# Borrowed PSUM banks at the outset, joined runs of small matmuls, inputs' loads on GpSimd's queue, and a last tile stored in halves, in a feed-forward plus S4 convolution kernel

## The chip, the cores and the metric

The kernel runs on one core of a Trainium2 chip. The metric is the device time of one launch in microseconds (us), the median of several launches. Engines are named as the profile names them: PE is TensorE, DVE VectorE, ACT ScalarE, POOL GpSimd, SP SyncE. SP, ACT and POOL also issue DMA transfers, each on a queue of its own; PSUM is the small memory that PE writes its results to, in banks, and SBUF the memory that all engines work from.

## The reference

The output is the input plus two branches of its layer norm: an S4 convolution over the sequence and a feed-forward network with silu.

```python
def _A_ref(u, A_re, A_im, B_re, B_im, C_re, C_im, log_dt, Dskip):
    dt = jnp.exp(log_dt)[:, None]
    logdA = dt * (A_re + 1j * A_im)
    dB = dt * (B_re + 1j * B_im)
    P = jnp.exp(logdA[:, :, None] * l[None, None, :])
    K = jnp.einsum("dn,dnl,dn->dl", Cc, P, dB).real
    ...
    y = irfft(rfft(u, padded) * rfft(K, padded))[:L]
    return y + u * Dskip

def _B_ref(x, w1, w2):
    return einsum("bsf,fd->bsd", silu(einsum("bsd,df->bsf", x, w1)), w2)

x = A_u
xn = _layernorm(x, axis=-1)
return x + _A_ref(xn, ...) + _B_ref(xn, B_w1, B_w2)
```

The sequence has L = 2048 rows of D = 576 columns, the hidden width F is 4608, each column has N = 128 complex states.

## The kernel before

**The feed-forward network** carries the bulk of TensorE's work. Every float32 factor is split into a high and a low part that TensorE takes at its fast float32 rate, and a product is the sum of three: high by high, high by low, low by high. The sequence is cut into four blocks of 512 rows, two to a half; the hidden width into nine chunks of four slices t = 0 to 3, 128 wide. For each half, each chunk and each of its two blocks:

- `up(blk, t)` (L305) makes one slice of the hidden layer: 14 matmuls into one bank `ph` (L313 to L315) from the transposed inputs xh, xl, x4 and the weights w1h, w1l; then ACT reads the bank with silu into gf (L321) and makes gh, its high part (L322), and DVE makes gl, its low part (L323). `ph` lies in the pool ps1, of two banks.
- `down(blk, jj)` (L325) multiplies by w2: for each 128-row tile, 12 matmuls for each of the two column halves into a bank `po` of the pool ps2, of three banks (L338), then DVE adds the bank to the accumulator acc (L342).

Only the first block's ups are done in two halves of 256 columns, all four t with columns 0 to 256 first (a = 0, e = 256), then all four with 256 to 512, since its second half of inputs arrives later.

**The outset** is what must happen before that runs: `load_x` (L162) brings tiles of 128 input rows, two at a time (tiles 0 and 1 apart), `phase0` (L204) and `norm` (L179) normalise them (statistics on DVE at L186, the power on POOL at L191, the result xn on DVE at L195 or on ACT at L200), and `put_xt` (L120) transposes them on PE (L124, L128) and splits them into xh on ACT (L125) and xl on DVE (L126). `load_w1` (L253) and `split_w1` (L272), `load_w2` (L286) and `split_w2` (L294) bring the weights and split them, the high part on ACT (L280, L300), the low part on DVE (L282, L302). `idle(n)` issues n matmuls of zeros (L857), which nobody reads, while the first inputs arrive.

**The side work** makes the convolution by a transform and is woven between the feed-forward matmuls. `kgen()` (L562) makes the convolution's kernel K in 18 rounds: DVE and ACT compute tables S and C, PE multiplies them in a run of 128 matmuls `kp` of 32-column tiles (L674), ACT copies the result to kt (L681), PE transforms it in a run of 16 matmuls `z` of 64-row tiles (L689), ACT copies these to `stage` (L697), and every second round SP stores `stage` to d1k in HBM (L702). `spread()` (L139) makes the inputs' transform in 16 steps j with two halves m each: the load xr (L145), a split sp on ACT and DVE (L150, L151), matmuls pu (L155, L156), the copy u1 on ACT (L157), and a store to d1u on POOL's queue (L158). `spectral()` (L708) reads d1k and d1u back and multiplies. `next_xt` (L349) loads the second half's transposed inputs on POOL's queue (L352, L355) and `split_xt` (L358) splits them. `tail()` and `add_conv` bring the convolution into acc, and `store` (L174) writes the tiles out; the last two tiles, 14 and 15, are written by the last lines of the program, each in four parts over SP and ACT.

**The order.** Each engine and each queue works through its instructions in the order in which the build put them, and a queue's transfer starts when its wait is met. The build's scheduler chooses this order from the program's, with a plan of times of its own. The kernel steers it with `behind(ins)`: what is issued inside stands behind the instruction `ins`, without a wait for it; the dictionary `pins` holds such instructions. `weave` hands the side work out among the feed-forward matmuls by marks.

## Time and profile before

| | |
|---|---|
| median of 3 runs | 1113.24 us (1112.6 to 1115.7) |
| the profiled execution | 1113.42 us, of which the span is 1111.6 |
| granted TensorE clock | 1.00 |
| PE busy | 1103.3 us, 99% of the span |
| DVE, ACT, POOL busy | 82%, 64%, 6% |
| moved by DMA | 148.56 MB, mean 134 GB/s |

The time is that of the launch; the span is what the profiler saw, from the first instruction to the last, and the difference lies around it. PE busy is the union of its matmuls' times, so a matmul that runs below its pace because the array changes its tiling counts as busy. Rows of a timeline give the start, the duration, the engine and line, the operation with its output and inputs, and in brackets the idle time ahead of it and what ended it. A run of like matmuls is folded into one row with its count; its duration is from the first start to the last end. The costliest groups by line are these: columns are the line, the engine and operation, the names, shapes and count, then busy us and mean ns, then the idle time just before them.

```profile
L338 PE MATMUL po<-w2l,gh 128*128 128x288 f32 x1152 | 338.5, 295 | 0.9 <-DVE w2l L302 0.9
L313 PE MATMUL ph<-xh,w1h 128*128 128x512 f32 (+1 forms) x592 | 162.1, 388 | 1.2 <-ACT gf L321 1.2
L674 PE MATMUL kp<-C 128*32 128x64 f32 x1152 | 35.2, 222 | 0.0
L689 PE MATMUL z<-f,kt 64*128 64x128 f32 x288 | 20.9, 285 | 0.0
```

### The profile page before, as it was taken

How to read it: one execution, taken by the hardware profiler on the slowest of the kernel's cores; microseconds unless marked ns; L12 is line 12 of the kernel's file. 1: busy time of each engine (PE TensorE's matmuls, PEld its weight loads, DVE VectorE, ACT ScalarE, POOL GpSimd, SP SyncE). 2: the span in 40 equal slices, each digit the busy share in tenths (PEclk: the TensorE clock that was granted, in tenths of full speed). 3: DMA queues.
4: the chain of work that ended last, by engine and by line, in shares of the span. 5: the costliest groups of instructions: out<-in, count | busy, mean ns of one | idle time of the engine just before them, and what ended most of it. 6: DMA issues, size and time to landing. Idle time of an engine off the chain costs nothing.

```text
span 1111.6 us, 22913 instructions
## 1 busy us (share of the span) xinstructions
PE 1103.3 (99%) x9168; PEld 997.8 (90%) x9168; DVE 916.9 (82%) x1546; ACT 709.2 (64%) x1228; POOL 69.8 (6%) x129
## 2 busy tenths in 40 slices
PE   8999999999999999999999999999999999999998
PEld 6998999899889899899989989999999999999887
DVE  6899899999999999999999837787778778784433
ACT  5574456676777676677866536877777878773210
POOL 1100000000000000011000000000000000000111
PEclk9999999999999999999999999999999999999999
DMA  9745522425242515255844163554545445434983
GB/s 258 201 122 152 137 71 61 120 63 130 82 107 80 134 61 131 77 149 161 219 123 105 44 173 106 169 157 128 161 145 150 139 146 171 129 107 130 248 211 86
DMA packets 175563, 148.56 MB, mean 134 GB/s; under 512 B 111024, under 2 KB 142272, under 8 KB 175328
## 3 DMA queue, kind: packets, MB, share of 16 engines
q1 hardware_dynamic: 165136, 112.33, 38.7%
q0 software_dynamic: 9568, 33.62, 9.5%
q8 instruction: 72, 1.18, 0.5%
q10 hardware_dynamic: 752, 1.15, 0.4%
q14 instruction: 35, 0.29, 0.1%
HBM read 102.53 MB, written 44.61 MB: 132 GB/s over the span
## 4 chain that ended last, share of the span: by engine, by line
PE 97%; DMA 1%; DVE 0%; SPq 0%; issue 0%; ACT 0%; ACTq 0%; POOL 0%; DVEq 0%
PE po L338 42%; PE ph L313 35%; PE kp L674 3%; PE ph L314 3%; PE ph L315 3%; PE pu L804 2%; PE pb L804 2%; PE pk L804 2%; PE z L689 2%; PE pu L155 1%; DMA acc<-in_A_u_dram 1%; PE py L825 1%; PE pu L156 1%; DMA w2r<-in_B_w_dram 0%; PE pt L124 0%; DVE st L186 0%
## 5 line engine op out<-in xcount | busy, mean ns | idle before, releaser
L338 PE MATMUL po<-w2l,gh 128*128 128x288 f32 x1152 | 338.5, 295 | 0.9 <-DVE w2l L302 0.9
L338 PE MATMUL po<-w2h,gl 128*128 128x288 f32 x1152 | 336.2, 295 | 0.0
L338 PE MATMUL po<-w2h,gh 128*128 128x288 f32 x1152 | 335.8, 295 | 0.0
L338 PEld LDWEIGHTS po<-w2h,gh 128*128 128x128 f32 x1152 | 215.1, 188 | 7.6 <-issue 2.8
L338 PEld LDWEIGHTS po<-w2l,gh 128*128 128x128 f32 x1152 | 215.9, 188 | 6.1 <-DVE w2l L302 1.1
L338 PEld LDWEIGHTS po<-w2h,gl 128*128 128x128 f32 x1152 | 215.4, 188 | 0.8
L321 ACT ACTIVATE gf<-ph 128x512 f32<-128x512 f32 (+1 forms) x148 | 86.4, 585 | 142.9 <-PE ph L315 128.3
L313 PE MATMUL ph<-xh,w1h 128*128 128x512 f32 (+1 forms) x592 | 162.1, 388 | 1.2 <-ACT gf L321 1.2
L313 PE MATMUL ph<-xl,w1h 128*128 128x512 f32 (+1 forms) x592 | 161.4, 386 | 0.0
L313 PE MATMUL ph<-xh,w1l 128*128 128x512 f32 (+1 forms) x592 | 161.0, 385 | 0.0
L342 DVE TENSOR_TENSOR acc<-po,acc 128x288 f32<-128x288 f32 x288 | 126.4, 452 | 37.4 <-PE po L338 36.1
L323 DVE TENSOR_TENSOR gl<-gf,gh 128x512 fp32r<-128x512 f32 (+1 forms) x148 | 99.2, 673 | 64.8 <-ACT gh L322 64.1
L313 PEld LDWEIGHTS ph<-xh,w1l 128*128 128x128 f32 x592 | 108.1, 188 | 19.9
L313 PEld LDWEIGHTS ph<-xl,w1h 128*128 128x128 f32 x592 | 108.0, 188 | 20.0 <-DVE xl L126 0.2
L313 PEld LDWEIGHTS ph<-xh,w1h 128*128 128x128 f32 x592 | 104.5, 188 | 18.5 <-ACT gf L321 1.8
L322 ACT CAST gh<-gf 128x512 fp32r<-128x512 f32 (+1 forms) x148 | 89.8, 609 | 10.1 <-PE po L338 7.1
L631 ACT ACTIVATE c<-th,magic 128x1040 f32<-128x1040 f32 x36 | 42.1, 1169 | 37.9 <-DVE C L654 28.0
L633 ACT ACTIVATE c<-th 128x1040 f32<-128x1040 f32 x36 | 38.7, 1075 | 34.0 <-DVE th L632 34.0
L300 ACT CAST w2h<-w2r 128x576 fp32r<-128x576 f32 x72 | 46.9, 671 | 17.2 <-PE po L338 14.9
L282 DVE TENSOR_TENSOR w1l<-w1r,w1h 128x640 fp32r<-128x640 f32 x72 | 57.1, 818 | 0.2
L314 PE MATMUL ph<-x,w1h 128*128 128x512 f32 (+1 forms) x148 | 57.0, 385 | 0.0
L315 PE MATMUL ph<-x,w1l 128*128 128x512 f32 (+1 forms) x148 | 56.9, 385 | 0.0
(184 smaller groups left out, 1830.1 us busy)
## 6 DMA issues: line engine op xcount, KB each, us to landing
w2r<-in_B_w_dram SPq DMA_DIRECT2D x72, 288.0 KB, 3.7
w1r<-in_B_w_dram SPq DMA_DIRECT2D x35, 512.0 KB, 3.9
d1u<-u POOLq DMA_DIRECT2D x32, 288.0 KB, 2.6
d1k<-stage SPq DMA_DIRECT2D x18, 512.0 KB, 6.8
ur<-d1u SPq DMA_DIRECT2D x32, 288.0 KB, 3.9
kr<-d1k SPq DMA_DIRECT2D x32, 288.0 KB, 2.8
d<-yo POOLq DMA_DIRECT2D x32, 288.0 KB, 3.7
ys<-d SPq DMA_DIRECT2D x32, 288.0 KB, 11.6
```

What stands on the lines that cost most here:

```text
L282: pins["w1l"] = nc.vector.tensor_sub(l1, src, h1).ins
L300: pins["w2h"] = nc.scalar.copy(h2, r2).ins
L313: nc.tensor.matmul(ph, w[:, kt, :], v[:, kt, a:e], start=n + kt == 0, stop=False)
L314: nc.tensor.matmul(ph, h1[:, 4, :], x4[:, a:e], start=False, stop=False)
L315: pins["pe"] = nc.tensor.matmul(ph, l1[:, 4, :], x4[:, a:e], start=False, stop=True).ins
L321: nc.scalar.activation(gf, ph, AF.Silu)
L322: pins["gh"] = nc.scalar.copy(gh, gf).ins
L323: pins["gl"] = nc.vector.tensor_sub(gl, gf, gh).ins
L338: pins["pe"] = nc.tensor.matmul(po[:, :HD], G[blk, t][g][:, js], W2[half, c, t][w][:, hs], start=n == 0, stop=n == 3 * FT - 1).ins
L342: nc.vector.tensor_add(acc[j][:, hs], po[:, :HD], acc[j][:, hs])
L631: nc.scalar.activation(c65, th, AF.Identity, bias=magic)
L804: nc.tensor.matmul(dst, st, mv[:, hs], start=n == 0, stop=n == 3 * len(terms) - 1)
```

## The change

Seven things are changed.

- `up`: the first halves of the slices t = 2 and 3 of the first block put `ph` into a bank of ps2, which the `po` of the downs use, rather than of ps1.
- `norm`: tile 3 is normalised on DVE (L195) rather than on ACT (L200), so its mb on DVE falls away.
- The loads of tiles 2 and 3 are issued on SP alone rather than on SP and ACT; of the first slices of w1, the two 64 KB rows that POOL issued go to SP and ACT. Eight idle matmuls rather than nine follow tile 0.
- What stands behind what: tiles 2 and 3 behind the latest w1l rather than the first; the w1l of slices 2 and 3 behind other steps of `norm`; the statistics of tiles 6 and 7 behind the latest w2l rather than the transposes of tile 3; the late tiles 8 and 9 behind an xn.
- `kgen`: the z run of a round is issued by `along` right behind the kp run of the next round rather than behind its own; kt gets two buffers; the last round's z stands alone.
- `spread`: the loads xr move from SP's queue to POOL's, and two steps are taken at every second round rather than one at each.
- `store`: tile 15 is written in two column halves, each in four parts over SP and ACT.

In the order that the build makes of it, 17 kp runs are followed directly by a z run, and the last z run stands in two parts with four matmuls of an up between them. On POOL's queue the load xr of step j + 1 stands between the two stores d1u of step j. Directly ahead of block 1's first up stand the five transposes of tile 7, where before 12 matmuls of a down stood between the fourth and the fifth. The last tile's stores are eight of 36 KB rather than four of 72 KB.

```diff
--- before.py
+++ after.py
@@ -142,7 +142,7 @@
         nc.gpsimd.dma_start(s1, cs1)
         for j in range(NJ):
             src = up.tile([P, D], F32, tag="xr", name="xr")
-            nc.sync.dma_start(src, dxn[:, j])
+            nc.gpsimd.dma_start(src, dxn[:, j])
             for m in range(2):
                 lo, hi = slice(64 * m, 64 * m + 64), slice(64 - 64 * m, 128 - 64 * m)
                 u1 = up.tile([P, D], F32, tag="u1", name="u1")
@@ -173,8 +173,9 @@
 
     def store(t, j, engines):
 
-        for ps, v, eng in quarters(ov, engines):
-            eng.dma_start(v[:, j:j + 2] if len(t.shape) > 2 else v[:, j], t[ps])
+        for hs in (slice(0, HD), slice(HD, D)) if j == NJ - 1 else (slice(0, D),):
+            for ps, v, eng in quarters(ov, engines):
+                eng.dma_start(v[:, j:j + 2] if len(t.shape) > 2 else v[:, j, hs], t[ps] if len(t.shape) > 2 else t[ps, hs])
 
     def norm(p0, js, xs):
 
@@ -187,11 +188,11 @@
             nc.vector.bn_aggr(out=mv[:, i, :], in_=st[:, i, :, :])
         sd = p0.tile([P, 2], F32, tag="sd", name="sd")
         mb = p0.tile([P, 2], F32, tag="mb", name="mb")
-        nc.vector.tensor_scalar(sd[:, :n], mv[:, :n, 1], 1e-5, None, op0=ALU.add)
+        pins["sdv"] = nc.vector.tensor_scalar(sd[:, :n], mv[:, :n, 1], 1e-5, None, op0=ALU.add).ins
         pins["sd"] = nc.gpsimd.tensor_tensor(sd[:, :n], sd[:, :n], mhalf[:, :n], op=ALU.pow).ins
         xn = p0.tile([P, 2, D], F32, tag="xn", name="xn") if js[0] < 8 else pairs[js[0]]
         for i, j in enumerate(js):
-            if j % 2 == 0 or j < 2:
+            if j % 2 == 0 or j < 4:
                 pins["xn"] = nc.vector.tensor_scalar(xn[:, i, :], xs[i], mv[:, i, 0:1], sd[:, i:i + 1],
                                                  op0=ALU.subtract, op1=ALU.mult).ins
             else:
@@ -203,11 +204,11 @@
 
     def phase0(p0, js, idle=None):
 
-        xs = load_x(js[0], accp, "acc", (nc.sync, nc.scalar) if js[0] < 4 else (nc.sync,))
+        xs = load_x(js[0], accp, "acc", (nc.sync, nc.scalar) if js[0] < 2 else (nc.sync,))
         acc.update(zip(js, xs))
         yield
         if js[0]:
-            with behind(pins["w1l0"] if js[0] == 2 else None):
+            with behind(pins["w1l"] if js[0] == 2 else None):
                 normed(p0, js, xs)
         else:
             for j, xj in zip(js, xs):
@@ -216,7 +217,7 @@
                 if not j:
                     pins["xt0s"] = pins["xt_s"]
                 with behind(pins["pt"]):
-                    idle(3 if j else 9)
+                    idle(3 if j else 8)
         pins[f"xt{js[1]}h"] = pins["xt_h"]
         pins[f"xt{js[1]}"], pins[f"xt{js[1]}s"] = pins["xt_v"], pins["xt_s"]
         yield
@@ -260,12 +261,12 @@
             v1 = w1[0:512, fs].rearrange("(k p) f -> p k f", p=P)
             eng = nc.sync
             if first and t == 0:
-                eng = nc.gpsimd
+                eng = nc.scalar
                 nc.sync.dma_start(r1[:, 0:2, :], v1[:, 0:2])
-                nc.scalar.dma_start(r1[:, 2:4, :], v1[:, 2:4])
+                eng.dma_start(r1[:, 2:4, :], v1[:, 2:4])
             else:
-                eng.dma_start(r1[:, 0:4, :], v1)
-            eng.dma_start(r1[0:64, 4, :], w1[512:576, fs])
+                nc.sync.dma_start(r1[:, 0:4, :], v1)
+            nc.sync.dma_start(r1[0:64, 4, :], w1[512:576, fs])
             pins["load"] = eng.dma_start(r1[64:128, 4, :], w1[512:576, fs]).ins
             R1[half, c, t] = r1
 
@@ -278,9 +279,8 @@
                 src = r1[:, :, i * P:(i + 1) * P]
                 with behind(pins.get("gh", pins["xt1s" if t + i else "xt0s"])):
                     nc.scalar.copy(h1, src)
-                with behind(pins["xn" if t else "xt1"] if first else None):
+                with behind(pins[("xn" if i else "sdv") if t else "xt1"] if first else None):
                     pins["w1l"] = nc.vector.tensor_sub(l1, src, h1).ins
-                pins.setdefault("w1l0", pins["w1l"])
                 W1[half, c, t + i] = h1, l1
 
         def load_w2(half, c, t):
@@ -299,7 +299,7 @@
             with behind(pins["xt_s"] if first else pins["gh"]):
                 pins["w2h"] = nc.scalar.copy(h2, r2).ins
             with behind(pins["w1l"] if first else None):
-                nc.vector.tensor_sub(l2, r2, h2)
+                pins["w2l"] = nc.vector.tensor_sub(l2, r2, h2).ins
             W2[half, c, t] = h2, l2
 
         def up(blk, t, a=0, e=512):
@@ -307,7 +307,8 @@
             half, c, b = blk
             xh, xl, x4 = xts[2 * half + b]
             h1, l1 = W1[half, c, t]
-            ph = ps1.tile([P, 512], F32, tag="ps1", name="ph")[:, a:e]
+            pool, tag = (ps2, "ps2") if e == 256 and t > 1 else (ps1, "ps1")
+            ph = pool.tile([P, 512], F32, tag=tag, name="ph")[:, a:e]
             for n, (w, v) in enumerate(((h1, xh), (h1, xl), (l1, xh))):
                 for kt in range(NKT):
                     nc.tensor.matmul(ph, w[:, kt, :], v[:, kt, a:e], start=n + kt == 0, stop=False)
@@ -618,6 +619,33 @@
                 return th
 
             stage = None
+            kts = []
+
+            def along(first):
+
+                nonlocal stage
+                i, kt = kts.pop(0)
+
+                z = [pss.tile([P, 512], F32, tag="pss", name="z") for _ in range(2)]
+                for eg in range(4):
+                    for h in (1, 0):
+                        rows = slice(64 * h, 64 * h + 64)
+                        with tc.high_priority(), behind(first):
+                            mm = nc.tensor.matmul(z[h][:, eg * P:(eg + 1) * P], kt[rows, eg * P:(eg + 1) * P], f1[rows],
+                                                  start=True, stop=True, tile_position=(64 * h, 0))
+                        first = first or mm.ins
+                r = (i - 1) % NRUN
+                if r == 0:
+                    stage = kg.tile([P, 64, NRUN * CH], F32, tag="stage", name="stage")
+                sv = stage[:, :, r * CH:(r + 2) * CH].rearrange("p k (e h c) -> p h e k c", h=2, c=2)
+                for h in range(2):
+                    nc.scalar.copy(sv[:, h], z[h].rearrange("p (e k c) -> p e k c", e=4, c=2))
+                if r == NRUN - 2:
+                    d0 = (i // NRUN) * NRUN * CH
+                    kv = d1k.rearrange("(k n) (g d) -> g n k d", n=64, g=2)
+                    for gp_ in range(2):
+                        nc.sync.dma_start(kv[gp_, :, :, d0:d0 + NRUN * CH], stage[gp_ * 64:(gp_ + 1) * 64])
+
             tabs = []
             nxt = head(0)
             al = powers(0)
@@ -677,29 +705,13 @@
                                 if begins:
                                     first = mm.ins
                 tabs = []
-                kt = kg.tile([P, 512], F32, tag="kt", name="kt")
+                if kts:
+                    along(mm.ins)
+                kt = kg.tile([P, 512], F32, tag="kt", name="kt", bufs=2)
                 nc.scalar.copy(kt, kp)
-
-                z = [pss.tile([P, 512], F32, tag="pss", name="z") for _ in range(2)]
-                first = None
-                for eg in range(4):
-                    for h in (1, 0):
-                        rows = slice(64 * h, 64 * h + 64)
-                        with tc.high_priority(), behind(first):
-                            mm = nc.tensor.matmul(z[h][:, eg * P:(eg + 1) * P], kt[rows, eg * P:(eg + 1) * P], f1[rows],
-                                                  start=True, stop=True, tile_position=(64 * h, 0))
-                        first = first or mm.ins
-                r = (i - 1) % NRUN
-                if r == 0:
-                    stage = kg.tile([P, 64, NRUN * CH], F32, tag="stage", name="stage")
-                sv = stage[:, :, r * CH:(r + 2) * CH].rearrange("p k (e h c) -> p h e k c", h=2, c=2)
-                for h in range(2):
-                    nc.scalar.copy(sv[:, h], z[h].rearrange("p (e k c) -> p e k c", e=4, c=2))
-                if r == NRUN - 2:
-                    d0 = (i // NRUN) * NRUN * CH
-                    kv = d1k.rearrange("(k n) (g d) -> g n k d", n=64, g=2)
-                    for gp_ in range(2):
-                        nc.sync.dma_start(kv[gp_, :, :, d0:d0 + NRUN * CH], stage[gp_ * 64:(gp_ + 1) * 64])
+                kts.append((i, kt))
+                if i + 1 == NCK:
+                    along(None)
                 yield (i + 1) / NCK
 
         nc.gpsimd.dma_start(d1k.rearrange("(k n) d -> n k d", n=P)[0],
@@ -867,7 +879,7 @@
                     next(p23)
                     yield 0
                     for js in ((4, 5), (6, 7)):
-                        with behind(pins["xt3"]):
+                        with behind(pins["xt3" if js[0] == 4 else "w2l"]):
                             for _ in phase0(pa, js):
                                 pass
                     kf["dt"] = steps()
@@ -881,7 +893,7 @@
 
                         xs = load_x(j, pb, "xj", (nc.sync,))
                         yield
-                        with behind(pins["gl"]):
+                        with behind(pins["xn" if j == 8 else "gl"]):
                             normed(pb, (j, j + 1), xs)
                         yield
 
@@ -896,7 +908,8 @@
             with tc.tile_pool(name="up", bufs=1) as up:
                 sp = spread(up)
                 for n, at in enumerate(kgen()):
-                    if n > 1:
+                    if n % 2 == 0 and n:
+                        next(sp, None)
                         next(sp, None)
                     yield marks[0] + at * (marks[1] - marks[0])
                 for _ in sp:
```

## The prediction

> **What bounds the kernel now.** I read the shares of busy time and the chain of waits first, then the busy time by stretch, then PE's timeline at the places that the change touches.
>
> ```profile
> span 1111.6 us, 22913 instructions
> PE 1103.3 (99%) x9168; PEld 997.8 (90%) x9168; DVE 916.9 (82%) x1546; ACT 709.2 (64%) x1228; POOL 69.8 (6%) x129
> ...
> PE 97%; DMA 1%; DVE 0%; SPq 0%; issue 0%; ACT 0%; ACTq 0%; POOL 0%; DVEq 0%
> ...
> 0.00:28.00 28.00, 24.32 (x149) 17.83 (x150) 18.48 (x49) 13.97 (x29) 3.78 (x10) 1.00 0.95 258
> 250.00:400.00 150.00, 150.00 (x1640) 134.68 (x1639) 148.17 (x221) 106.88 (x161) 5.93 (x11) 1.00 0.39 101
> ```
>
> The columns of the last two rows are the stretch, then busy PE, PE's weight loads, DVE, ACT and POOL, the granted clock, the DMA share and GB/s. TensorE sets the end: it is the chain but for 3%. In the first 28 us it is idle 3.7 us, with the transfers 95% busy. In 250 to 400 us it is never idle, its clock is full, and DVE is busy 148.17 of 150. So only two things can shorten the run: stalls of PE in the outset, and what PE itself spends. What lies outside PE at the end is the third, a microsecond or so. No matmul of the reference is added or removed; "PE busy" however contains the price of changing shape, which is where the joins aim.
>
> **Outset.** These are PE's rows (each with the idle time that the profile saw before it), then DVE's, ACT's and POOL's.
>
> ```profile
> 13.58 0.28 PE L315 MATMUL ph<-x,w1l 128*128 128x256 f32 x1
> 14.33 0.74 PE L313 MATMUL ph<-xh,w1h 128*128 128x256 f32 x4 [0.47 <-ACT gf L321]
> ...
> 16.75 0.74 PE L313 MATMUL ph<-xh,w1h 128*128 128x256 f32 x4 [0.47 <-ACT gf L321]
> ...
> 24.70 0.74 PE L313 MATMUL ph<-xh,w1h 128*128 128x256 f32 x4 [0.24 <-ACT gf L321]
> ...
> 26.35 0.28 PE L315 MATMUL ph<-x,w1l 128*128 128x256 f32 x1
> 27.49 0.40 PE L338 MATMUL po<-w2l,gh 128*128 128x288 f32 x1 [0.86 <-DVE w2l L302]
> ...
> 25.24 1.54 DVE L186 BATCH_NORM_STATS2 st<-acc 128x6 f32<-128x288 f32 x4 [2.00 <-DMA acc<-in_A_u_dram]
> 26.69 1.41 DVE L302 TENSOR_TENSOR w2l<-w2r,w2h 128x576 fp32r<-128x576 f32 x2
> ...
> 17.32 0.87 ACT L200 ACTIVATE xn<-acc,mb,sd 128x576 f32<-128x576 f32 x1 [0.19 <-DMA w2r<-in_B_w_dram]
> ...
> 6.81 0.82 DVE L186 BATCH_NORM_STATS2 st<-acc 128x6 f32<-128x288 f32 x2 [0.33 <-DMA acc<-in_A_u_dram]
> 8.74 0.58 DVE L195 TENSOR_SCALAR xn<-acc,mv,sd 128x576 f32<-128x576 f32 x1 [0.68 <-POOL sd L191]
> ...
> 1.95 0.55 POOL L268 DMA_DIRECT2D w1r<-in_B_w_dram  x1
> 2.48 0.54 POOL L269 DMA_DIRECT2D w1r<-in_B_w_dram  x1
> ```
>
> A 256-column matmul follows its neighbour after 0.12 us (four span 0.64, of which 0.28 is one: 0.36 over three). From 13.58 to 14.33 are 0.75, so 0.63 are lost (the bracket says 0.47, since ends are modelled; I add the same 0.16 elsewhere). The next two cost 0.63 and 0.40, and the wait for w2l costs 27.49 − 26.35 − 0.12 = 1.02. Together 2.68.
>
> The first two are waits for a bank: both ph banks are full until ACT has read one. With t = 2 and 3 in the idle po banks these waits have no cause, and I take 1.26 as gone. The third is a second half (a = 256), which stays on the old banks: some of its 0.40 stays. The fourth arises because DVE stands 2.00 us in statistics of tiles 6 and 7 whose rows have not landed, with w2l queued behind; pinned behind w2l, they cannot block it. But PE gets there earlier too, so w2l is needed earlier by what the others gave: of 1.02 I take 0.7 as gone. Tile 3 leaves ACT's 0.87 and costs DVE 0.58, the duration of such a row (at 8.74), less the small mb; I put both at 0, as DVE then waits for loads, not loads for DVE (+0.5 if it doesn't). Of the two rows of w1 on POOL, 128 KB at 258 GB/s hold the wire 0.5 us; they were issued ahead of what tile 1's statistics await at 6.81, and its xn at 8.74, its transposes and so the first real matmul hang on that. I take 0.3. One dummy matmul fewer covers nothing that waits. Sum: 1.26 + 0.15 + 0.7 + 0.3 = −2.4. The bounds: if the wire at 95% merely delivers w1 and w2 as late as before, only about 1.0 stays; if all goes, 2.68 + 0.3 = 3.0.
>
> **A wait that the change makes at 42 us.** In the changed order the five transposes of tile 7 stand directly ahead of block 1's first matmuls; before, twelve downs stood between:
>
> ```profile
> 41.82 0.60 PE L124 MATMUL pt<-ident,xn 128*128 128x128 f32 x4
> 42.18 0.38 PE L338 MATMUL po<-w2h,gh 128*128 128x288 f32 x1
> ...
> 42.46 0.59 ACT L125 CAST xh<-pt 128x512 fp32r<-128x512 f32 x1 [0.71 <-PE pt L124]
> ```
>
> The cast starts 0.64 after the first transpose and ends 0.59 later, at 43.05; PE, free from 42.18 plus the fifth transpose (about 0.11), would stand 0.76 for it. I take +0.65 (0.3 to 0.9).
>
> **The joins.** Each of the 18 rounds (one kt copy each) has one kp run and one z run, each between full-array matmuls:
>
> ```profile
> 306.37 0.40 PE L313 MATMUL ph<-xh,w1h 128*128 128x512 f32 x1
> 306.70 0.34 PE L674 MATMUL kp<-C 128*32 128x64 f32 x8
> ...
> 308.46 0.31 PE L674 MATMUL kp<-S 128*32 128x64 f32 x6
> 308.70 0.40 PE L338 MATMUL po<-w2h,gh 128*128 128x288 f32 x1
> ...
> 313.84 1.07 PE L313 MATMUL ph<-xl,w1h 128*128 128x512 f32 x4
> 314.84 1.16 PE L689 MATMUL z<-f,kt 64*128 64x128 f32 x16
> 315.93 0.40 PE L155 MATMUL pu<-sp,s 128*128 128x288 f32 x1
> 316.17 0.30 PE L156 MATMUL pu<-sp,s 128*128 128x288 f32 x1
> ...
> L681 ACT COPY kt<-kp x18: 561/572/588, 172.5 to 640.5; 128x512 f32<-128x512 f32 x18
> ```
>
> A 512-column matmul is followed after 0.227 at pace (x4: 1.07 − 0.39 over three). Into z: the last of the x4 starts at 313.84 + 0.68 = 314.52, z at 314.84, so 0.09 more than pace; into kp: 306.70 − 306.37 − 0.23 = 0.10. Out of kp: the last of x6 (0.22 long) starts at 308.55, the full matmul at 308.70: 0.15. Out of z: the last starts near 315.73, so 0.20. And the first full matmul is followed after 0.24 where 0.133 is the pace: 0.105. A join of kp and z takes away one exit (0.15 + 0.105) and one entry (0.09) and puts one change kp to z in. No row shows that. If it costs an exit of kp, 0.15, a join saves 0.195; if nothing, 0.34; if as much as leaving and entering, nothing. I take 0.195: the row of an exit from the same 32-column tiles is the nearest. 17 joins save 3.3; the changed order splits the last z in two around four ups, one excursion more at 0.09 + 0.20 + 0.105 = 0.39. So −2.9, from +0.4 to −5.4. Beside it: the Trainium skill, "TensorEngine Tiling (Array Packing)", Key Properties, says that changing the tiling mode drains TensorE. That speaks for a price at kp to z too and against the free join; with one drain at an exit's price the term is the −2.9 above, with a full one it is the rival's.
>
> z now comes a round later, behind the next kp run; its kt (two buffers) has long been ready, and its stage copies on ACT move by a round. At the end the last z, its stage, the stores of d1k and the loads of kr must fit in before the spectral matmuls, and the changed order leaves some 4 us less of main work between (about 27, an estimate from the counts of matmuls there at the paces above). I put no wait for it; if the cover fails, PE waits for kr what is missing, up to 1 us.
>
> **Loads moved to POOL, and what queues behind them.**
>
> ```profile
> xr<-dxn SPq DMA_DIRECT2D x16, 288.0 KB, 2.9
> d1u<-u POOLq DMA_DIRECT2D x32, 288.0 KB, 2.6
> xl<-dxt POOLq DMA_DIRECT2D x2, 1024.0 KB, 7.9
> r<-dxt POOLq DMA_DIRECT2D x4, 128.0 KB, 7.6
> ...
> 494.89 0.77 POOL L352 DMA_DIRECT2D xl<-dxt  x1 [5.04 <-PE ph L313]
> 506.25 1.15 ACT L362 CAST xh<-xl 128x512 fp32r<-128x512 f32 x2
> ```
>
> The 16 xr loads stand on POOL between two d1u stores, and each d1u waits for ACT's u1. As d1u on POOL lands in 2.6 and xr on SP in 2.9, the queue alone changes nothing; by rows I put 0. The Trainium skill, "DMA: Bandwidth & Descriptors", Issuing engine by pattern, gives simple loads to Sync and calls that path generally faster; these two rows of one size do not bear it out. What does change is the lead: the cast sp on ACT follows the issue by some 4 to 8 us of main work in the changed order (an estimate from the same counts). ACT, 107 busy of 150, covers a short stand. The six loads of next_xt (1 MB and 128 KB) take 7 to 8 us; the casts of xl, at 506.25 before, 11.4 us after the issue at 494.89, now stand some 7 us behind it and ahead of a w2h cast for which PE waits: 0 to 1.2 us, I take 0.6. With 0.2 for the rest (DVE's 1.2% of idle time in 250 to 400 us leaves no room for shifted work): +0.8, from 0 to +3.
>
> **End.**
>
> ```profile
> 1107.04 0.46 DVE L342 TENSOR_TENSOR acc<-po,acc 128x288 f32<-128x288 f32 x1 [1.14 <-PE po L338]
> 1107.52 0.78 SPq L177 DMA_DIRECT2D out_dram<-acc  x2
> 1107.53 0.85 ACTq L177 DMA_DIRECT2D out_dram<-acc  x2
> out_dram<-acc SPq DMA_DIRECT2D x4, 72.0 KB, 1.8
> ```
>
> The last tile goes out in four stores, two a queue. In halves the first four leave earlier, but four still follow the last add, two a queue at 0.4 us an issue, each half the size. Only their bytes shrink: −0.15 (0 to −0.3).
>
> **Sum.** The profiled execution took 1113.42 (span 1111.6, 1.8 around it). −2.4 + 0.65 − 2.9 + 0.8 − 0.15 = −4.0: 1109.4. The median shown is 1113.24, 0.2 less; so 1109.2.
>
> **Rivals.** *The join is free* (kp to z like matmuls of one mode): 17 × 0.34 − 0.39 = 5.4, 2.5 more: 1106.7. For it, both shapes are part tiles; against it, every other change of shape in the rows costs. *The join saves nothing*: kp to z costs what leaving and entering do, 0.34 in all, and the extra excursion 0.39: +0.4 instead of −2.9, 1112.5. For it, the two runs differ in rows and columns of their tiles; against it, an entry (0.09) and an exit (0.25) each price a change to or from the full array, and here is only one change. That is the rule of the tiling page in the Trainium skill at its hardest: every change of mode drains in full. *The outset is only shifted*: the wire and DVE's chain hold PE at w1, w2l and xh instead of the banks, and 1.75 net becomes 0: 1111.0. For it speaks the 95%; against it, that no PE wait there names a DMA. *Thin loads make it slower*: xr, queued on POOL with d1u, next_xt and their waits, comes later than its cast; ACT stands in order at sp, behind it gf, and with two ph banks PE waits. It decides once issue to landing passes some 6 us, as the POOL rows at 7.6 and 7.9 do and the 2.6 does not. Half of the 16 loads 1.5 us late for PE cost 12 us, the other terms give −4.8 (the forecast without its +0.8): 1113.2 + 7.2 = 1120.4. From 8 us of such waits on, it is slower by what can be measured. For it stand the rows at 7.6 and 7.9, against it ACT's idle third, and that PE is idle nowhere in 250 to 400 us.
>
> **Chances.** Forecast 0.50 (1107.6 to 1110.9); free join 0.15; no saving by joins 0.10; shifted outset 0.11; thin loads 0.14. What a measurement here can tell from no change is 0.3%, 3.3 us, so faster means below 1109.9. That takes 0.41 of the forecast's 0.50 and the free join: 0.56. Within: 0.09 + 0.10 + 0.11 and 0.02 of thin loads: 0.32. Slower 0.12. The range, 1106.6 to 1112.5, leaves out the slow case and the ends.
>
> **What would show it.** Right: no idle at 14.3 and 16.7 us, none before po near 27; PE through the eight half-ups and the first downs of the first block about 2 us sooner; kp and z in one run of about 2.9 us with 0.15 between, PE busy lower by some 3 us; a gap of about 0.7 near 41 us. Wrong: a kp-to-z gap of 0.3 or 0.02; PE waiting for ACT gf, kt or w2h after 170 us, with sp or xh casts waiting for a DMA ahead of them; xr above 6 us; more than 1 us of PE idle between the last z and the first spectral matmul.

## The result, and the profile after

The changed kernel takes 1117.59 us in the median of 22 runs (1115.32 to 1122.04), the kernel before 1113.79 (1112.49 to 1116.53): slower by the ratio 1.0034, 95% interval 1.0027 to 1.0041. Forecast was 1109.2, some 4 us faster. The profiled execution took 1117.55, its span is 1115.8.

These are the shares of busy time and the chain of waits of the changed kernel, from its page, and behind them a stretch of its busy time (columns as in the prediction).

```profile
span 1115.8 us, 22956 instructions
PE 1103.0 (99%) x9167; PEld 999.3 (90%) x9167; DVE 917.3 (82%) x1546; ACT 705.7 (63%) x1227; POOL 78.5 (7%) x143
...
PE 72%; DVE 14%; issue 6%; ACT 4%; DMA 3%; SPq 1%; POOL 0%; DVEq 0%; ACTq 0%; POOLq 0%
```

```profile
400.00:680.00 280.00, 276.19 (x2779) 249.84 (x2779) 242.23 (x368) 179.94 (x274) 18.68 (x33) 1.00 0.47 125
```

PE is as busy as before (1103.0 against 1103.3), but the span is 4.2 us longer, and the chain, 97% PE before, now runs through DVE for 14% and through ACT and transfers for 7%: PE has begun to wait for others. The waits stand in PE's timeline; these are its rows with a bracket from 17 us on, and among them the joined run of one round and the last z run.

```profile
17.67 0.66 PE L124 MATMUL pt<-ident,xn 128*128 128x128 f32 x4 [0.20 <-DVE xn L196]
21.20 0.74 PE L314 MATMUL ph<-xl,w1h 128*128 128x256 f32 x4 [0.24 <-DVE xl L126]
24.95 0.40 PE L339 MATMUL po<-w2l,gh 128*128 128x288 f32 x1 [0.70 <-DVE w2l L302]
...
43.67 0.50 PE L314 MATMUL ph<-xh,w1h 128*128 128x512 f32 x1 [0.56 <-ACT xh L125]
...
198.62 0.31 PE L702 MATMUL kp<-S 128*32 128x64 f32 x6
198.87 1.16 PE L634 MATMUL z<-f,kt 64*128 64x128 f32 x16
199.96 0.40 PE L339 MATMUL po<-w2h,gh 128*128 128x288 f32 x1
200.19 0.30 PE L339 MATMUL po<-w2l,gh 128*128 128x288 f32 x1
...
233.47 0.40 PE L339 MATMUL po<-w2h,gl 128*128 128x288 f32 x1 [0.41 <-DVE gl L324]
235.38 0.97 PE L314 MATMUL ph<-xh,w1h 128*128 128x512 f32 x3 [0.45 <-ACT w1h L281]
444.98 0.53 PE L339 MATMUL po<-w2h,gh 128*128 128x288 f32 x2 [1.47 <-ACT w2h L300]
504.50 0.53 PE L339 MATMUL po<-w2h,gh 128*128 128x288 f32 x2 [0.51 <-ACT w2h L300]
568.97 0.40 PE L339 MATMUL po<-w2h,gh 128*128 128x288 f32 x1 [1.13 <-ACT w2h L300]
570.41 0.40 PE L155 MATMUL pu<-sp,s 128*128 128x288 f32 x1 [0.25 <-ACT kt L711]
573.96 0.73 PE L314 MATMUL ph<-xh,w1h 128*128 128x512 f32 x2 [0.45 <-ACT gf L322]
...
651.73 1.16 PE L634 MATMUL z<-f,kt 64*128 64x128 f32 x8
653.94 1.16 PE L634 MATMUL z<-f,kt 64*128 64x128 f32 x8
...
1040.27 1.13 PE L837 MATMUL py<-ys,s 64*32 64x288 f32 x25 [0.86 <-DMA ys<-d]
```

As in the prediction, what is lost is the distance of two starts less the pace, a little more than the bracket. Laid side by side at equal amounts of PE's work, the two traces differ so:

| part | predicted | measured |
|---|---|---|
| outset, up to the first kp run (its own wait at 43 us, +0.73, included) | −1.75 | 0.0 |
| joins: 17 × 0.202 saved | −3.3 | −3.4 |
| last z run in two parts | +0.39 | +1.3 |
| waits of PE between 170 and 650 us | +0.8 | +5.9 |
| wait of the first py for ys | – | +0.9 |
| after the last matmul | −0.15 | −1.0 |

With 0.5 of small rest this is the 4.2 of the spans. The granted clock of this execution was 1.00. From the last matmul's start to the last landing it went from 3.25 to 2.92; the other 0.7 of the last row lie behind that landing.

### The profile page after: what moved, and what is told of

The parts are those of the page before. It is cut to its first block, busy times and chain, and to the rows that moved or that the text cites. A ratio compares the mean times of both kernels' runs of the same rounds, so it can differ in the third digit from the quotient of the medians.

```text
span 1115.8 us, 22956 instructions
## 1 busy us (share of the span) xinstructions
PE 1103.0 (99%) x9167; PEld 999.3 (90%) x9167; DVE 917.3 (82%) x1546; ACT 705.7 (63%) x1227; POOL 78.5 (7%) x143
## 4 chain that ended last, share of the span: by engine, by line
PE 72%; DVE 14%; issue 6%; ACT 4%; DMA 3%; SPq 1%; POOL 0%; DVEq 0%; ACTq 0%; POOLq 0%
PE po L339 30%; PE ph L314 26%; PE ph L316 2%; PE ph L315 2%; PE pu L816 2%; PE pk L816 2%; PE pb L816 2%; PE kp L702 2%; DVE C L670 2%; DVE acc L343 1%; DVE S L681 1%; DVE th L616 1%; DVE gl L324 1%; DVE C L681 1%; DMA w2r<-in_B_w_dram 1%
```

## The experiments

The first four take the parts apart, each on the kernel before. Their times stand beside 1113.39 us for the kernel before.

**The outset alone**: the hunks in load_x, norm, phase0, split_w1, split_w2, up and the pins.

```diff
+            pool, tag = (ps2, "ps2") if e == 256 and t > 1 else (ps1, "ps1")
...
+            if j % 2 == 0 or j < 4:
```

> The kernel before with the outset's parts alone (borrowed banks, tile 3 on DVE, loads and pins of the outset). The trace of the full change shows waits for banks gone (1.26 us) but new waits for xn, xl and xh (0.36 + 0.18 + 0.40 + 0.73) in their place, and w2l still 0.87 late. Theory A (the outset is bound by its loads and DVE's chain, so the gain only moves): 0 us against before, within 0.5. Theory B (the outset gains and what follows loses): 1.5 to 2 us faster. The rows to look at: the time at which block 1's first up starts, 43.9 before.

Measured: 1112.92 us, ratio 0.9994 (0.9985 to 1.0002), not to be told from before. In its profile PE is 0.9 ahead of before when block 1 begins, and loses 0.83 at 75 us. The time is theory A's; the cause isn't, since a gain does get through the outset and is lost behind ACT. ACT's rows there, in this run and in the kernel before:

```profile
71.58 2.13 ACT L515 ACTIVATE r<-r 128x2304 f32<-128x2304 f32 x1
73.73 1.28 ACT L321 ACT_TABLE_LOAD   x1
75.02 0.60 ACT L321 ACTIVATE gf<-ph 128x512 f32<-128x512 f32 x1
```

```profile
70.77 2.12 ACT L515 ACTIVATE r<-r 128x2304 f32<-128x2304 f32 x1
72.91 1.28 ACT L321 ACT_TABLE_LOAD   x1
74.21 0.60 ACT L321 ACTIVATE gf<-ph 128x512 f32<-128x512 f32 x1
```

The silu that empties the ph bank stands behind an exponential and a table load that belong to the convolution; they come 0.8 later than before while PE comes 0.9 earlier.

**The joined runs alone**: `along` and the second kt buffer; xr stays on SP, one step a round.

```diff
+                if kts:
+                    along(mm.ins)
```

> The kernel before with the joined runs alone; loads of the inputs' transform stay on SP, one step a round. PE's own saving is 17 x 0.20 = 3.4, less the last z run, which in two parts costs 1.29 more: 2.1. Theory D (DVE, 97% busy between the first and the last kp run, sets the pace there): PE waits give back what it saved, 0 to +2 us against before. Theory L (the moved loads and the two steps make the waits): no such waits here, 2 us faster, or 1 faster if the late last z costs the py run 0.9.

Measured: 1118.96 us, 1.0044 (1.0032 to 1.0056): slower than before by itself, with no load moved. Theory L fell for this part. The longest wait of its profile, on PE, and the ACT rows that end it:

```profile
392.54 0.40 PE L155 MATMUL pu<-sp,s 128*128 128x288 f32 x1 [1.28 <-ACT kt L710]
...
389.69 1.36 ACT L280 CAST w1h<-w1r 128x640 fp32r<-128x640 f32 x2
390.96 1.06 ACT L660 ACTIVATE c<-th 128x1040 f32<-128x1040 f32 x1
391.92 0.56 ACT L710 COPY kt<-kp 128x512 f32<-128x512 f32 x1
```

A joined run fills all three small banks: one kp, two z. The pu that follows needs one, and the first to come free is kp's, when ACT has copied it; ACT has other work first. Four such waits sum to 4.1 us, all waits after 170 us to 6.6.

**The inputs' transform alone**: its loads on POOL, two steps at every second round.

> The kernel before with the inputs' transform alone changed: its loads on POOL's queue and two steps at every second round; kp and z apart. Theory L: the waits of the full change (5.9 us between 230 and 575) are here, 4 to 6 us slower. Theory D: with PE no faster than before, DVE keeps up but for the doubled rounds: 0 to 2 us slower.

Measured: 1119.66 us, 1.0064 (1.0045 to 1.0082). The numbers are theory L's, but not its rows:

```profile
447.81 0.40 PE L338 MATMUL po<-w2h,gh 128*128 128x288 f32 x1 [2.14 <-ACT w2h L300]
...
443.26 1.00 SPq L291 DMA_DIRECT2D w2r<-in_B_w_dram  x2
442.48 1.42 DVE L302 TENSOR_TENSOR w2l<-w2r,w2h 128x576 fp32r<-128x576 f32 x2
...
1040.65 1.24 PE L825 MATMUL py<-ys,s 64*32 64x288 f32 x32 [1.81 <-DMA ys<-d]
```

No xr stands in these chains. The raw rows of w2 have two buffers, and the third load of a chunk waits until DVE has made w2l of the first. DVE gets to that at 442.48, SP issues at 443.26, the data land 3.8 later, ACT casts them, PE goes on at 447.81. The other half of the loss is the first py, which waits for ys.

**The store in halves alone**:

> The kernel before with the last tile stored in halves alone. In the trace of the full change the last landing comes 2.92 us after the last matmul's start rather than 3.25, and the span ends 0.95 after it rather than 1.64. If both are the halves' doing: 1.0 us faster; if only the landing: 0.3 faster; the rest as before, as no other instruction moves.

Measured: 1113.06 us, 0.9994 (0.9986 to 1.0003); the span 1111.3 against 1111.6. It gives 0.3 at most.

The joins and the transform alone lose 5.6 and 6.3 us, together with the rest 3.8: the losses do not add. The next four (beside 1113.59 for before) try single causes.

**Three w2 buffers** in the full change; kt gets one buffer to make room.

```diff
-            r2 = (...).tile([P, D], F32, tag="w2r", name="w2r", bufs=2)
+            r2 = r2p.tile([P, D], F32, tag="w2r", name="w2r", bufs=3 if r2p is wp else 2)
...
-                kt = kg.tile([P, 512], F32, tag="kt", name="kt", bufs=2)
+                kt = kg.tile([P, 512], F32, tag="kt", name="kt")
```

> The full change with three buffers for w2's raw rows in place of two, and one for kt in place of two (for the space). Theory C (a chain: DVE, full, makes w2l late; only then is w2's buffer free, SP issues the load 3.4 us ahead of ACT's cast, and PE waits for w2h): the third load no longer waits for a w2l of the same chunk, the waits for w2h at 443, 503 and 567 us (1.63 + 0.67 + 1.29) and what they pull after them are gone, 3 to 5 us faster than the full change, so -1 to +1 against before. Theory L (the loads are late because the moved xr loads and the queues delay them): the waits stay, 1.003 of before.

Measured: 1117.72 us, 1.0040 (1.0025 to 1.0055): no change in time, though the waits for w2h (444.98, 504.50 and 568.97 in the rows above) are gone, and the last z is whole. The stage of the rounds, which costs the full change 4.4 us against before (from 160 to 650 us of work), costs 0.7 here. But the py row now reads:

```profile
1039.27 1.24 PE L838 MATMUL py<-ys,s 64*32 64x288 f32 x32 [2.40 <-DMA ys<-d]
```

What PE gained it lost there, and 0.8 at 75 us as in the outset alone. At py it lost more than the longer wait: from 1040.52 the granted clock is 0.50 for 3.4 us, which costs PE half of that, 1.7. The profiled launch, with this one stretch, has a mean granted clock of 0.998, and all five launches show 0.997 or 0.998, where those of the kernel before show 0.999 or 1.000.

**The low part of the inputs' split on POOL** in the full change (`nc.gpsimd.tensor_sub(sp[hi, :], ...)`).

> The full change with the low part of the inputs' split (L151, 32 instructions of 0.75 us) on POOL in place of DVE. Theory D (DVE sets the pace between the first and the last kp run): with 24 us less of 476 DVE keeps up, the waits for w2h and gl between 230 and 575 us are gone and the joins' saving shows: 4 to 6 us faster than the full change, -2 to 0 against before. Theory L: no change, 1.003. A POOL instruction slower than some 3 us would hold the d1u stores and xr loads behind it.

Measured: 1135.44 us, 1.0198 (1.0154 to 1.0241). It tells nothing of DVE, since POOL needs 1976 ns in the median where DVE needed 753, and up to 5140; PE's waits behind 170 us sum to 19 us, 3.42 of them once for this instruction itself, and the clock is halved three times for 3.4 us.

**Four small banks, two po banks**, with the join alone and without it.

```diff
-    ps2 = ctx.enter_context(tc.tile_pool(name="ps2", bufs=3, space=PSUM))
-    pss = ctx.enter_context(tc.tile_pool(name="pss", bufs=3, space=PSUM))
+    ps2 = ctx.enter_context(tc.tile_pool(name="ps2", bufs=2, space=PSUM))
+    pss = ctx.enter_context(tc.tile_pool(name="pss", bufs=4, space=PSUM))
```

> The kernel before with the joined runs alone and four small PSUM banks (pool pss) and two po banks rather than three and three. In the run of the join alone PE waits 0.79, 0.55, 1.43 and 1.29 us for ACT's kt copy ahead of pu: kp and two z fill all three small banks, and pu needs one. Theory P (banks): with a fourth these waits are gone and the last z run is whole, 5 to 7 us faster than the join alone, 0 to -2 against before. Rival: two po banks make PE wait for DVE's adds instead, at no gain or a loss.

> The kernel before with four small banks and two po banks, nothing else: the control of the run with the join. If two po banks suffice, PE shows no wait for DVE's add to a po bank and the time is that of before, within 1 us; if not, the waits show ahead of the first po matmul of a tile, 144 tiles by up to 0.1 us.

Measured: 1157.95 and 1150.81 us, 1.0403 and 1.0337. The rival came true: without the join PE waits 10.2 us for DVE's add to a po bank (17 times) and 8.5 for gf. So the control fell, and theory P isn't tested by this pair; no pu waits for kt any more, but far more is lost elsewhere.

The next four stand beside 1113.78 for before.

**xr back on SP** in the full change, one word changed; PE, ACT and DVE keep their orders.

> The full change with the loads xr back on SP's queue; the orders on PE, ACT and DVE are those of the full change, only two queues differ. Theory L (queues and moved loads make the waits): the waits at 233, 443, 503 and 567 us shrink, 3 to 6 us faster than the full change, -2 to +1 against before. Theory C/D (DVE's order and fullness hold w2's buffers, banks and gl): the same waits at the same places, 1.003 of before, within 1 us of the full change.

Measured: 1123.39 us, 1.0096 (1.0080 to 1.0112): 5.8 slower than the full change. Neither theory expected that. Part of it is the clock, halved in three stretches of its profile, which is its slowest launch. On SP the load stands in order among w1, w2 and stores; ACT's cast then waits for it, with what is behind the cast:

```profile
525.58 0.67 ACT L150 CAST sp<-xr 64x576 fp32r<-64x576 f32 x1 [4.91 <-DMA xr<-dxn]
```

In the full change, on POOL, xr lands after 3.0/3.3/6.3 us (least, median, most), and ACT waits for it six times, 5.6 us in all, 1.6 at the longest. So with two steps at once the loads are better off on POOL.

**The join alone with three w2 buffers**, and the same with outset and store.

> The kernel before with the joined runs alone, three buffers for w2's raw rows and one for kt. In this order the pu stand 3 us or more behind a joined run (1.2 to 3.6 in the join alone) and the last z run is whole. Theory P+C (the join costs through banks that only ACT's kt copy frees, and w2's buffers): PE waits between 170 and 650 us fall from 6.6 to under 3, so that the stage is 1 to 3 us shorter than before. As only 18.0 us of main work lie between the last spectral matmul and the first py (22.2 before), py then waits 1 to 2.5 us for ys: total 0 to -2 against before. Theory D (DVE's 97% set the pace): the waits come back elsewhere, +1 to +4.

> As the run before (join, three w2 buffers, one kt), with the outset's parts and the store in halves added. If the outset's and the store's gains are real (each 0.06% faster alone, within noise), 0.3 to 0.7 us less than the run before; the wait at 75 us behind ACT's exponentials and table load takes back what the outset gains.

Measured: 1118.89 us, 1.0047 (1.0034 to 1.0060), and 1115.45, 1.0025 (1.0014 to 1.0037). The waits of the stage fall to 2.8 in the first, and PE reaches the spectral stage 0.2 us ahead of before; since it came into the stage 0.5 ahead, these waits and 0.9 of smaller ones have taken all of the joins' 3.4. Then the first py run costs 5.06 and 4.45 us where 1.36 is bare: a wait of 2.48 and 2.15, and in both the clock at 0.50 for 3.4 us from 1037.41. Theory P+C holds for the waits of the stage, not for its time, which was to be 1 to 3 us shorter than before and is 0.3 longer; and its price for py was too small.

**The kernel before with three w2 buffers**, the control.

> The kernel before with three buffers for w2's raw rows alone, the control: kp and z apart, nothing moved by hand, but the order that the build makes has 18.0 us of main work between the last spectral matmul and the first py in place of 22.2. If the late wait of the full change for ys comes of this order alone: 1 to 2.5 us slower than before by a wait ahead of the first py, and none between 170 and 650 us. Rival (the late wait comes of the joined or doubled steps): as before, within 0.5.

Measured: 1114.45 us, 1.0012 (1.0003 to 1.0021). Nothing waits between 170 and 650 us, and py does:

```profile
1036.63 1.24 PE L826 MATMUL py<-ys,s 64*32 64x288 f32 x32 [1.30 <-DMA ys<-d]
```

So the late wait needs neither join nor moved load; what this kernel shares with the full change is the order with 18 us of main work between the last spectral matmul and the first py. In the kernel before 22.4 us pass there, without a wait.

The last batches: beside 1113.87 and, for the last two, 1113.66 for before.

**The first py one step later** in the full change, and in the best try.

```diff
-        tail_at = (0.91, 0.934, 0.967, 0.0072)
+        tail_at = (0.91, 0.938, 0.967, 0.0072)
```

> The full change with the first py run placed one chunk step later (its mark 0.934 becomes 0.938), nothing else. If the late wait of the full change (0.93 us in its profile, up to 3.7 in others) comes only of the 18 us of main work that the order leaves between the last spectral matmul and the first py, it is gone here: 1 to 2 us faster than the full change (1115.5 to 1116.6). Rival (the loads ys take as long whenever they start, or the rest of the tail is squeezed): no change.

> The best try (join, three w2 buffers, one kt, outset, store in halves; loads on SP, one step a round) with the first py run one step later. Its py run cost 4.4 us where 1.36 is bare: 2.5 to 3.1 us faster than the best try, so 1112.3 to 1113, 0.5 to 1.5 faster than before. If py's wait only moves to the next py run: no change.

Measured: 1117.58 us, 1.0032 (1.0020 to 1.0044): no gain in the full change, though py's wait is gone; in that profile the wait for w2h near 567 us is 2.83 in place of 1.29, with the same order, and behind it the clock is halved. These are that wait, the stretch at half clock and what follows; the clock is the third number from the end:

```profile
566.40:569.10 2.70, 0.06 (x1) 0.00 (x0) 0.64 (x1) 0.70 (x2) 0.00 (x0) 1.00 0.37 137
570.25:573.66 3.41, 3.16 (x14) 3.09 (x14) 3.41 (x5) 3.41 (x6) 0.00 (x0) 0.50 0.38 106
573.66:577.00 3.34, 3.34 (x18) 2.85 (x18) 2.77 (x6) 3.29 (x8) 0.54 (x1) 1.00 0.73 126
```

Seven of its eight launches show a mean clock of 0.998 or less, as the profiled one does; the eighth, at 1.000, took 1113.69, level with before. That points to the wait for w2h and the clock behind it as what takes the gain back, though one launch is little to go by. In the best try 1112.67, 0.9992 (0.9984 to 1.0001): 2.8 less, as expected, and level with before.

**Both waits off in the full change**: three w2 buffers, one kt, the first py later.

> The full change with three w2 buffers, one kt, and the first py one step later: both kinds of wait taken off together. With three buffers alone the profile had 2.6 us of waits between 170 and 650 us (5.9 in the full change) and 3 us more at the first py; with the py later alone the time was the full change's. Theory C+O (the loss is these two waits, each of which hides the other): 3 to 4 us faster than the full change, 0 to +1 against before. If other waits take their place: 1.003 of before.

Measured: 1113.13 us, 0.9994 (0.9985 to 1.0003). Each alone gave nothing in the median, both together 4.5 us, the whole loss and a little. Not all of the 4.5 is the two waits: the order that the build makes here has the last z run whole as well, which by the trace is worth 1.3, and none of its eleven launches shows a clock under 0.999. Its span is 1111.5; a stretch of its busy time:

```profile
400.00:680.00 280.00, 278.95 (x2795) 251.89 (x2794) 246.52 (x374) 181.89 (x281) 18.68 (x33) 1.00 0.50 128
```

In 400 to 680 us PE is idle 1.05 us, 3.81 in the full change.

**The rounds stretched** over more main work, in the best try with the later py.

```diff
-        marks = (0.13, 0.597, 0.823)
+        marks = (0.13, 0.604, 0.823)
```

> As the run before, with the end of the rounds' stretch at mark 0.604 in place of 0.597, so that the same 18 rounds lie over 1.6% more main work. Theory D (in 420 to 570 us DVE's work of a round is longer than PE's, and PE waits): the waits of the best try there (0.47 + 0.23 + 0.42 + 0.31 + 0.91) shrink to under 1 us, another 1 to 2 us faster than the run before. Theory O (they are accidents of an order): others of the same size take their place.

> As the best try with the first py later, with the rounds' stretch ending at mark 0.610 (0.604 in the run before, 0.597 in the kernel). Theory D: DVE has still more main work to hide behind, waits between 400 and 640 us under 1 us, 1 to 2 us faster than the best try with the first py later (1112.7). Against it: the spectral stage gets shorter by the same and starts later, and at some point its loads are late for py; then 1113 to 1116.

Measured: 1114.31 us (1111.23 to 1118.06), 1.0006 (0.9994 to 1.0017) at 0.604, and 1117.38, 1.0039 (1.0023 to 1.0055) at 0.610. In the profile of the first, which is its fastest run, no wait stands between 400 and 530 us and PE is some 3 ahead of before at 480, 1.1 from the outset and the rest from the joins so far; then two waits take 2.2 at 537 and 539, for the banks of z and po. In the second PE waits 3.1 for w1h at 537, whose raw rows ACT had stood 5.88 us for, with the clock halved behind it, and 1.8 before a later py. Theory D isn't borne out by the times, and its opposite isn't either.

## Why the prediction was wrong

**The join's own price was right.** From the last kp start (198.62 + 0.09 = 198.71) to z are 0.16, and I had taken 0.15 from the exit row; a join saves 0.202 against 0.195. Neither the free join nor the full price came.

**The last z was mis-sized.** I priced the split as one more excursion, 0.39. But 16 matmuls of z run in pairs, one on each half of the rows; the eight of one half take 1.16 us (651.73), as the sixteen do (198.87). Two halves apart cost a whole run more, 1.29. The Trainium skill, "TensorEngine Tiling (Array Packing)", Key Properties, says that tiles work independently, in parallel; these rows agree.

**The outset was only shifted**, the rival at 0.11. The bank waits are gone as argued (1.26). But w2l still costs 0.87, of which I had taken 0.7 as gone: DVE does it right behind the statistics of tiles 4 and 5, which wait for their load like those of 6 and 7 before. And DVE's xn and xl now end waits of 0.94 in sum, while the first real matmul came 0.16 later, not 0.3 sooner. The 0.65 at 42 us was right (0.73). Where some gain does get through, ACT's exponential and table load at 75 us take it.

**The step that failed is the +0.8 for new waits in the middle**, which measured 5.9, and 0.9 at py, for which I had no term. I saw that DVE had 1.2% of idle time, named it, and then put 0.2 for it. Two chains that I had not priced make up most of these waits. One is w2's raw buffers, 3.6 of the 5.9: they free only when DVE has made w2l, and behind that stand SP's issue, the transfer and ACT's cast. These are its rows ahead of PE's wait at 568.97:

```profile
562.90 1.43 DVE L302 TENSOR_TENSOR w2l<-w2r,w2h 128x576 fp32r<-128x576 f32 x2
564.37 0.84 SPq L291 DMA_DIRECT2D w2r<-in_B_w_dram  x2
568.24 0.67 ACT L300 CAST w2h<-w2r 128x576 fp32r<-128x576 f32 x1 [7.55 <-DMA w2r<-in_B_w_dram]
```

At 444.98 the transfer took 3.4 us, here 3.9, and 7.7 ahead of 504.50, while next_xt's loads were under way. My 0.6 for the casts of next_xt is near the 0.67 lost at 504.50, but by luck: these casts had ended 0.8 before the data of w2 landed. The other chain is the loads ys, for which the changed order leaves 18 us where 22 stood. With three w2 buffers the waits for w2h are gone, with the later py that for ys; taken off together the change is level with before. That nothing else has a part in the 4.5 us is not shown, since the last z run became whole with it. The 2.3 of the 5.9 that PE waited for gl, w1h, kt and gf were not tried by themselves. A third chain, small banks that only ACT's kt copy frees, costs 4.1 in the join alone and 0.4 in the full change.

**A wait can cost more than its length**, and I had no term for that either. Of the 22 launches of the full change ten show a mean clock of 1.000, with a median of 1116.7, and twelve 0.997 or 0.998, with 1118.4. The 1.7 between them is what one stretch of 3.4 us at half clock costs. The profiled execution is one of the ten, so its 4.2 holds no such stretch. Taken off singly, each wait left the other long enough to halve the clock in the profile, which is a part of why the medians showed no gain.

**The slower rival got the sign, not the cause.** It had the moved xr loads come late and pass 6 us. They take 3.3 in the median and 6.3 once at most, and with xr on SP the change loses 5.8 more. That the queue alone costs nothing is not shown: no run moves the loads without the double steps.

**The store** gave 0.3 or less by itself, as forecast. The other 0.7 behind the last landing of the full change did not come with it, and their cause stays open.

**Open.** Whether a fuller DVE would in itself bound the stage: with the two chains off, the full change and the best try are level with before, so the joins' 3.4 us still do not show, and stretching the rounds did not settle it. A version with pu kept off the joined runs by order alone wasn't tried. None of the versions is faster than before beyond its interval; 1112.67 comes nearest.

## What to carry to other kernels

In a kernel whose bound engine never waits, saved time on that engine is worth only the slack of every chain that feeds it, and these slacks are read one by one: from the reader back to the buffer's release, the engine that releases, the queue that issues. When a scheduler makes the order, a small edit redraws all of it, and a part tried alone may lose more than the whole; take waits off in pairs before calling one of them harmless, since the next one hides it. A wait of two or three microseconds on PE can halve its clock for a while: here that added 1.7 us. A run of part-array matmuls that work side by side must not be split by the tile: each half costs the whole.

## What the runs showed of the hardware

POOL took 1976 ns in the median, 5140 at most, for the subtraction of 64 × 576 that took DVE 753. The Trainium skill, "GPSIMD Engine Reference", 4.1 Engine selection, gives about twice for two inputs; here it is 2.6 times, with DVE at work beside it. The Trainium skill, "GPSIMD Engine Reference", 1. Specifications, says that its access to SBUF is shared with DVE; no run here separates that.

The same run shows the granted clock halved after one long wait of PE:

```profile
374.20:377.80 3.60, 0.33 (x3) 0.10 (x1) 3.60 (x6) 1.14 (x1) 3.60 (x1) 0.99 0.00 0
377.80:378.90 1.10, 0.95 (x4) 0.95 (x5) 1.10 (x4) 0.04 (x2) 0.66 (x2) 0.50 0.00 0
378.90:381.10 2.20, 2.20 (x7) 1.81 (x7) 1.19 (x2) 0.78 (x2) 0.54 (x1) 0.50 0.47 134
381.10:384.00 2.90, 2.90 (x19) 2.61 (x19) 0.06 (x1) 2.50 (x4) 1.43 (x1) 0.99 0.26 102
```

PE is idle for all but 0.33 of 3.6 us, then the clock (third number from the end) is 0.50 for 3.3 us, then full again: the wait costs some 1.6 us more than its length. Shorter waits did the same: 2.7 us in the full change with the later py, 2.1 in the best try, 1.6 once with xr back on SP, each followed by 3.4 us at half clock. One of 2.1 in the inputs' transform alone left the clock at 1.00, as did those of the profiled full change, 1.6 us at most; so the length of a wait alone doesn't decide. The Trainium skill, "TensorE: Matmul & The Clock Gate", Part 1, names windows of about 3.4 us for both ways; the way back up agrees, the way down came after less idle time in these runs.
